# One core, attention and MLP: the same work in another written-out order on every engine

## The chip, the cores and the metric

The kernel runs on one core of a Trainium2 chip. The core has TensorE (PE, matrix products), VectorE (DVE), ScalarE (ACT), GpSimd (POOL) and SyncE (SP). SP computes nothing, it only issues transfers; ACT and POOL can issue transfers too. Each engine works through its own list in order, and a wait for a semaphore at the head of a list holds up all that stands behind it. The metric is the device time of one execution in microseconds.

## The reference

There are two parts. The first is an attention with positive random features, for 8 batches of 8 heads, 576 positions and 64 dimensions:

```
phi(x) = exp(omega x - |x|^2/2 - max) / sqrt(128)      # x = q or k, scaled
kv[m,d] = sum_s phi(k)[s,m] v[s,d];   z[m] = sum_s phi(k)[s,m]
attn[s,d] = phi(q)[s,:] kv[:,d] / (phi(q)[s,:] z + 1e-6)
```

Its output, 4608 tokens of 512 values, goes through an MLP: h = x w_in (512 to 2048), g = h clip(h+3, 0, 6)/6, out = g w_out (2048 to 512). All inputs and the output are float32.

## The kernel before

**Stages.** The program is a list of about 1960 operations, built by `op(...)` calls and numbered in that order. Batches 0 to 7 go through the attention. Of each batch, 512 tokens make one block of the MLP; the 64 left over of every batch are woven into a ninth block (8). TensorE does the attention of one batch while it does the MLP of the block before.

**Names.** An operation's name ends in its batch or block and a number within it. In the attention of batch b and head pair m:

- `k00.b`, `v00.b`, `v10.b`, `ql0.b`, `vl.b` and so on are the loads (line 622). From batch 1 on, k and q are cast to bfloat16 on the way, by loads that POOL issues; v comes as float32 by SP. `castk`, `castq` are the casts of batch 0.
- `T` are TensorE's transposes of k and q in batches 0 and 1 (line 535), `Tev` the copies of their results out of PSUM. From batch 2 on `Tdmak`, `Tdmaq` are transposing transfers on SP's queue (line 748).
- `K`, `Q` are the products with omega in batches 0 to 2 (lines 811, 831). From batch 3 on they come in four bursts `R` a batch, with 64 rows (lines 767, 770). `eK`, `eQ` are the exponentials on ACT, `mx` the maxima on DVE, `cc` their reciprocals.
- `vc`, `vcc`, `vcl` are v and a column of ones scaled by those reciprocals (lines 941 to 949, 857, 860), for the main tokens and the left-over ones. `kv` is the product of phi(k) and v (lines 957, 959), `kvz` its copy, `num`, `rec` and `div` make the quotient (lines 985, 997, 1001).
- `X` turns the quotient on TensorE (line 538) in batches 0 and 1; later `Xdma` (line 1030) and, for the left-over tokens, `Sdma` (line 887) do that on SP's queue.

In the MLP:

- `mm1` is x w_in (line 1054; 1199 for block 0; 1133, in seven products of quarters in place of eight, for blocks 7 and 8), followed by `relu` on ACT and `g` on DVE. In those last blocks `s1`, `s2`, `s3` copy parts of a product within PSUM, `a1`, `a2` add on DVE, and `X1` to `X4` are sums of the inputs.
- `mm2` is g w_out of block 0 (line 1224). From block 1 on it is done in seven products `P1.0` to `P1.6` (the first number is the block, line 1312; 1381 for the last product of block 8). They need sums and differences of g's quarters, `S1` to `S4` (line 1240, nearly all on POOL), and their parts are put together by `p1`, `u2`, `u3`, `C11` to `C22` (ACT or DVE). `out`, `outw`, `outl` are the stores.

w_in comes in pieces `wi0` to `wi3` (line 595), w_out in `wo0` to `wo7` (line 604), through POOL's queue.

**What sets the order.** `ORDER` (line 19) holds one list of operation numbers for each engine, 110 to 550 numbers long. `Prog.schedule` takes the operation at the head of each list, always the one that can begin first by the planner's own clock, and so fixes three things: the program, the PSUM slot (of eight, `Ring`) that an operation gets, and where TensorE's idle fillers (`idle`, line 576, products of ones that nobody reads) stand in the first 21 us. A transfer costs its queue the time `issue` in that clock, and its data share the transfer engines by the weight `packet`. `Prog.emit` then derives the waits from the dependencies. On the chip an engine's list runs in the given order, whatever the clock said. An operation that may run on several engines runs on the one whose list holds its number.

**Gates.** Loads of later batches wait for something that is done by then: those of batch 2 for pieces of w_out (`kb` for wo4, `qb` for wo5, v for wo7), those of batch b from 3 on for products of block b - 2. SP's and POOL's queues hold such a load, and all behind it, until its gate opens.

Of the kernel before, what the change touches and what calls it, by code (L numbers as in the profile page):

```python
# [20 lines left out]
        13, 118, 139, 156, 124, 144, 150, 162, 115, 168, 147, 127, 153, 121, 159, 165, 136, 130, 133, 177, 185, 175,  # L21
        183, 197, 187, 142, 212, 179, 181, 199, 204, 214, 171, 227, 242, 202, 217, 229, 244, 219, 410, 416, 173, 189,
        417, 232, 404, 254, 247, 405, 222, 234, 406, 207, 249, 407, 257, 411, 412, 418, 413, 419, 422, 280, 425, 252,
        237, 260, 428, 300, 431, 434, 437, 440, 286, 284, 282, 443, 318, 306, 303, 288, 446, 449, 309, 312, 452, 298,
        296, 455, 315, 324, 294, 345, 458, 290, 575, 292, 321, 353, 576, 577, 327, 341, 335, 585, 586, 337, 339, 587,
        595, 588, 596, 331, 605, 366, 333, 578, 329, 579, 597, 355, 589, 590, 379, 598, 591, 368, 371, 592, 392, 580,
        581, 343, 606, 599, 381, 358, 607, 384, 600, 582, 394, 397, 601, 374, 608, 361, 609, 602, 387, 400, 610, 611,
        612, 638, 514, 626, 506, 629, 512, 623, 641, 632, 653, 504, 508, 499, 647, 644, 662, 656, 659, 484, 475, 487,
        496, 478, 481, 674, 668, 520, 518, 490, 493, 677, 510, 516, 671, 784, 785, 528, 502, 794, 533, 540, 530, 787,
        545, 542, 800, 564, 552, 788, 717, 554, 795, 569, 566, 557, 797, 798, 697, 801, 803, 804, 710, 807, 808, 811,  # L30
        817, 826, 724, 820, 737, 814, 832, 841, 829, 835, 739, 742, 749, 844, 847, 850, 761, 862, 856, 859, 773, 754,
        865, 778, 766, 751, 972, 988, 775, 973, 763, 982, 975, 976, 983, 885, 985, 986, 989, 898, 991, 992, 1005, 999,
        1014, 1002, 995, 996, 1017, 905, 1008, 1023, 1020, 1029, 925, 1035, 1032, 912, 1038, 1044, 937, 1050, 927,
        1047, 949, 1053, 939, 942, 930, 1160, 1161, 1176, 954, 961, 1170, 966, 951, 963, 1163, 1171, 1086, 1164, 1173,
        1174, 1073, 1177, 1179, 1180, 1093, 1202, 1193, 1190, 1187, 1183, 1184, 1100, 1205, 1196, 1113, 1208, 1217,
        1211, 1118, 1220, 1223, 1125, 1226, 1115, 1137, 1127, 1235, 1130, 1139, 1238, 1232, 1142, 1149, 1241, 1348,
        1349, 1151, 1364, 1154, 1351, 1274, 1352, 1358, 1359, 1281, 1365, 1361, 1362, 1390, 1375, 1378, 1381, 1367,
        1368, 1393, 1371, 1372, 1384, 1405, 1261, 1399, 1414, 1396, 1420, 1411, 1408, 1426, 1301, 1313, 1429, 1303,
        1318, 1306, 1536, 1315, 1423, 1325, 1537, 1288, 1552, 1539, 1540, 1327, 1546, 1330, 1547, 1462, 1337, 1549,
        1342, 1339, 1550, 1553, 1469, 1555, 1556, 1476, 1559, 1560, 1449, 1563, 1569, 1566, 1572, 1581, 1501, 1593,  # L40
        1506, 1503, 1489, 1584, 1525, 1494, 1578, 1491, 1530, 1527, 1513, 1587, 1518, 1596, 1515, 1599, 1602, 1614,
        1608, 1611, 1617, 1631, 1632, 1662, 1675, 1634, 1665, 1691, 1678, 1667, 1635, 1680, 1704, 1670, 1694, 1641,
        1720, 1696, 1683, 1642, 1707, 1699, 1723, 1709, 1733, 1644, 1645, 1725, 1712, 1749, 1736, 1650, 1738, 1728,
        1762, 1752, 1651, 1741, 1754, 1809, 1765, 1647, 1648, 1812, 1767, 1822, 1757, 1654, 1814, 1655, 1770, 1825,
        1817, 1838, 1827, 1778, 1779, 1841, 1851, 1830, 1843, 1867, 1781, 1854, 1782, 1846, 1856, 1880, 1870, 1788,
        1872, 1859, 1883, 1789, 1885, 1909, 1875, 1794, 1896, 1791, 1792, 1888, 1899, 1795, 1912, 1901, 1941, 1914,
        1797, 1798, 1904, 1917, 1801, 1935, 1925, 1926, 1802, 1936, 1928, 1929, 1938, 1939, 1942, 1960, 1957, 1945,
        1946, 1954,
    ],
    "SP": [  # L50
        0, 21, 17, 23, 19, 22, 25, 24, 31, 27, 32, 26, 28, 29, 30, 269, 270, 271, 474, 473, 472, 471, 470, 468, 690,
        469, 402, 614, 584, 694, 696, 594, 693, 695, 692, 604, 536, 548, 560, 572, 691, 573, 881, 878, 810, 883, 879,
        806, 745, 757, 781, 769, 882, 782, 880, 884, 1069, 998, 1072, 1066, 1070, 1071, 994, 1068, 933, 945, 970, 957,
        969, 1067, 1260, 1259, 1257, 1258, 1186, 1133, 1121, 1145, 1157, 1182, 1254, 1158, 1256, 1255, 1374, 1370,
        1447, 1445, 1446, 1448, 1309, 1443, 1333, 1321, 1345, 1444, 1346, 1442, 1509, 1497, 1533, 1521, 1562, 1558,
        1534, 1653, 1657, 1800, 1804, 1953, 1952, 1959, 1962, 1950, 1956,
    ],
    "ACT": [
        18, 20, 117, 119, 157, 145, 151, 163, 132, 169, 148, 129, 154, 193, 166, 196, 160, 178, 211, 184, 137, 176,
        186, 225, 182, 180, 243, 188, 172, 218, 174, 190, 223, 408, 414, 420, 423, 281, 426, 238, 208, 429, 253, 432,  # L60
        301, 435, 438, 441, 283, 285, 444, 261, 319, 307, 304, 447, 310, 450, 313, 289, 299, 352, 297, 325, 346, 316,
        453, 291, 293, 354, 322, 328, 342, 336, 338, 456, 340, 332, 378, 367, 334, 391, 330, 459, 390, 380, 344, 593,
        583, 362, 375, 388, 401, 613, 507, 515, 630, 627, 624, 513, 642, 633, 639, 654, 505, 509, 500, 648, 645, 603,
        663, 657, 660, 476, 497, 482, 479, 485, 675, 488, 494, 519, 669, 491, 523, 511, 672, 517, 503, 529, 539, 678,
        521, 551, 550, 553, 565, 720, 718, 723, 722, 706, 703, 704, 700, 708, 698, 403, 713, 711, 716, 715, 736, 709,
        812, 702, 748, 818, 747, 729, 821, 727, 815, 725, 730, 827, 833, 830, 836, 759, 842, 848, 845, 851, 863, 857,
        774, 860, 866, 974, 977, 897, 894, 891, 896, 892, 888, 886, 899, 890, 903, 921, 901, 1000, 1006, 1003, 923,
        1015, 1018, 906, 936, 904, 1009, 1024, 908, 1021, 911, 1030, 910, 1036, 1033, 913, 574, 915, 1039, 1045, 918,
        938, 1051, 1048, 917, 1054, 959, 960, 962, 1091, 1087, 1092, 1089, 1079, 1084, 1076, 1082, 1074, 1078, 1080,
        1085, 1098, 1099, 1094, 1096, 1194, 1191, 1108, 1203, 1188, 1112, 1111, 1206, 1103, 1197, 1105, 1101, 1209,  # L70
        1212, 1124, 1136, 1218, 1221, 1106, 1224, 1126, 1227, 1138, 1147, 1148, 1239, 1233, 1236, 1242, 1350, 1277,
        1280, 1279, 1275, 1284, 1287, 1282, 1376, 1353, 1379, 1391, 1382, 1286, 1312, 1394, 1385, 1406, 1262, 1270,
        1268, 1266, 1400, 1264, 1415, 1267, 1397, 1297, 1412, 1273, 1409, 1272, 1427, 1324, 1421, 1323, 1430, 1538,
        1424, 1293, 1291, 1289, 1541, 1336, 1294, 1338, 1468, 1465, 1463, 1467, 1474, 1472, 1470, 1159, 1475, 1479,
        1477, 1482, 1481, 1450, 1452, 1458, 1456, 1564, 1455, 1570, 1567, 1454, 1488, 1573, 1502, 1461, 1582, 1460,
        1490, 1585, 1526, 1579, 1514, 1594, 1588, 1597, 1603, 1600, 1609, 1615, 1612, 1618, 1633, 1663, 1664, 1676,
        1677, 1666, 1692, 1679, 1671, 1693, 1636, 1673, 1695, 1684, 1705, 1706, 1686, 1722, 1708, 1700, 1724, 1702,
        1713, 1734, 1735, 1715, 1750, 1737, 1729, 1731, 1753, 1763, 1742, 1764, 1744, 1758, 1810, 1813, 1823, 1760,
        1771, 1824, 1773, 1826, 1818, 1820, 1839, 1831, 1842, 1780, 1852, 1853, 1847, 1833, 1783, 1849, 1860, 1881,
        1882, 1862, 1884, 1876, 1878, 1897, 1889, 1891, 1900, 1913, 1905, 1918, 1907, 1920, 1927, 1930, 1948, 1949,  # L80
        1951,
    ],
    "DVE": [
        16, 12, 11, 15, 14, 5, 138, 4, 9, 140, 10, 125, 7, 158, 146, 116, 191, 152, 164, 6, 122, 128, 149, 155, 194,
        209, 134, 167, 170, 131, 161, 141, 239, 224, 198, 143, 200, 213, 201, 205, 215, 216, 228, 203, 206, 230, 245,
        231, 220, 246, 221, 233, 255, 248, 235, 236, 250, 258, 256, 251, 409, 415, 259, 421, 424, 8, 427, 1623, 430,
# [316 lines left out]
def _emit(nc, es, q, k, v, omega, w_in, w_out, out):  # L403
# [136 lines left out]
    def turned(vx, b, n):  # L540
# [4 lines left out]
       issue=0.4)  # L545
# [67 lines left out]
    def load(b, eng, gates):  # L613
        pb = b % 2
# [3 lines left out]
        def dma(part, dst, src, n, keys, gate, prio, run):  # L618
            cast = b > 0 and part[0] in "kq"
# [4 lines left out]
               name="%s.%d" % (part, b), issue=0.85 if cast else 0.47 if b else 0.52, packet=50.0 if run == 1024 else 18.0)  # L624
# [877 lines left out]
```

The softmax here doesn't subtract the row's maximum and nothing guards it: scores larger than these inputs give would overflow.

## Time and profile before

| quantity | value |
|---|---|
| median of 5 runs | 303.73 us (303.01 to 304.05) |
| profiled execution, its own time | 304.34 us |
| its span, first to last instruction | 302.5 us |
| matmuls on TensorE | 2800, 65 of them fillers |
| granted TensorE clock | 1.00 in every slice |
| VectorE, ScalarE, GpSimd busy | 247.4, 214.3, 237.4 us |
| transposing transfer kT or qT, SP's queue | 1.35 and 1.38 us each, median |
| transposing transfer xT, SP's queue | 1.27 us each, median |
| bytes read and written | 36.73 and 9.44 MB |

In the timelines a row is the start in us, the duration, engine, line, operation, what it writes and reads, the shape and the count; at its end stands the idle time of the engine before it and what released it. SPq and POOLq are the sequencers. Rows of equal operations that follow each other are merged. A matmul's row runs to the end of its result, so that TensorE looks busy between two matmuls whose starts are a little further apart than their columns need.

### The profile page before, as it was taken

The numbers are of one execution on the slowest core, as the hardware profiler recorded it, in microseconds if no ns is written. First come the engines' busy times: TensorE is split into PE (matmuls) and PEld (weight loads), VectorE is DVE, ScalarE is ACT, GpSimd is POOL, SyncE is SP. The second block draws the span as 40 slices with busy tenths as digits, with TensorE's granted clock in tenths as the row PEclk, the third lists the DMA queues.
The fourth block names the chain that finished last, engine by engine and source line by source line (L and its number), as shares of the span: only waits on it lengthen the run. The fifth ranks groups of instructions, "written<-read, shape, count | busy, mean of one in ns | idle before, by whom it ended". The sixth has DMA issues, their size and how long they took to land.

```text
span 302.5 us, 7410 instructions
## 1 busy us (share of the span) xinstructions
PE 296.1 (98%) x2800; PEld 211.0 (70%) x2800; DVE 247.4 (82%) x547; ACT 214.3 (71%) x516; POOL 237.4 (78%) x255
## 2 busy tenths in 40 slices
PE   8999999999999999999999999999999999999995
PEld 5678955545776568655865586657756688888884
DVE  3889897859988794879878967687798999999875
ACT  4898996579949963799479854697686687575400
POOL 2883776069897999799969996998959999999990
PEclk9999999999999999999999999999999999999999
DMA  7999999999994996799949969898932500110034
GB/s 239 286 188 177 265 188 113 194 179 144 221 229 96 137 238 170 154 163 226 177 120 137 161 158 237 114 218 129 134 95 52 168 1 2 69 73 2 0 141 140
DMA packets 90100, 44.89 MB, mean 148 GB/s; under 512 B 57936, under 2 KB 87760, under 8 KB 90064
## 3 DMA queue, kind: packets, MB, share of 16 engines
q1 hardware_dynamic: 62496, 31.04, 45.5%
q0 software_dynamic: 26592, 12.46, 33.7%
q10 hardware_dynamic: 976, 0.92, 0.9%
q8 instruction: 22, 0.36, 0.5%
q14 instruction: 14, 0.11, 0.2%
HBM read 36.73 MB, written 9.44 MB: 153 GB/s over the span
## 4 chain that ended last, share of the span: by engine, by line
PE 90%; ACT 3%; DVE 2%; DMA 2%; POOL 1%; SPq 1%; issue 0%; POOLq 0%
PE p L1312 32%; PE p L1054 28%; PE p L1133 8%; PE p L1224 4%; PE p L985 3%; PE p L1199 3%; PE p L957 3%; PE p L767 2%; DMA q<-in_q_dram 2%; PE p L770 2%; PE p L831 1%; DVE mx L822 1%; PE p L811 1%; ACT kp L818 1%; ACT vc L943 1%; SPq L622 1%
## 5 line engine op out<-in xcount | busy, mean ns | idle before, releaser
L1054 PE MATMUL p<-xT,wi 128*128 128x512 f16 x384 | 89.9, 380 | 0.0
L1062 DVE SCALAR_TENSOR_TENSOR gT<-tsb,p 128x512 f16<-128x512 f16 x96 | 62.2, 676 | 12.8 <-ACT tsb L1060 12.2
L1060 ACT ACTIVATE tsb<-p 128x512 f16<-128x512 f32 x96 | 55.4, 606 | 14.7 <-PE p L1054 8.9
L1054 PEld LDWEIGHTS p<-xT,wi 128*128 128x128 f16 x384 | 35.7, 98 | 38.5 <-issue 1.1
L1312 PE MATMUL p<-wo,gT 128*128 128x256 f16 x368 | 45.3, 273 | 0.0
L1240 POOL TENSOR_TENSOR gT<-gT 128x512 f16<-128x512 f16 x32 | 37.0, 1155 | 3.2 <-DVE gT L1062 0.9
L1312 PEld LDWEIGHTS p<-wo,gT 128*128 128x128 f16 x368 | 34.9, 98 | 6.4 <-issue 1.1
L1240 POOL TENSOR_TENSOR s<-gT 128x512 f16<-128x512 f16 x31 | 36.2, 1168 | 3.9 <-DVE gT L1062 1.7
L1240 POOL TENSOR_TENSOR s<-gT,s 128x512 f16<-128x512 f16 x31 | 35.9, 1156 | 2.6 <-DVE gT L1062 0.3
L1240 POOL TENSOR_TENSOR gT<-gT,s 128x512 f16<-128x512 f16 x30 | 34.7, 1155 | 2.3
L791 DVE TENSOR_REDUCE mx<-kp 128x4 f32<-128x512 bf16 (+1 forms) x50 | 29.7, 622 | 6.5 <-ACT kp L786 6.4
L795 ACT ACTIVATE qpT<-p 128x512 bf16<-128x512 f32 (+1 forms) x50 | 27.5, 571 | 7.7 <-PE p L770 7.1
L622 POOL DMA_DIRECT2D qb<-in_q_dram x28 | 19.6, 716 | 16.4 <-PE p L1054 15.9
L1312 PE MATMUL p<-t,gT 128*128 128x256 f16 x256 | 31.6, 273 | 0.0
L786 ACT ACTIVATE kp<-p 128x512 bf16<-128x512 f32 (+1 forms) x50 | 26.2, 568 | 7.5 <-PE p L770 7.5
L941 POOL TENSOR_TENSOR vc<-v,cc 128x512 bf16<-128x512 f32 x22 | 23.4, 1064 | 10.0 <-DVE mx L822 3.6
L1001 DVE TENSOR_TENSOR xb<-p,rec 128x256 f16<-128x256 f32 (+1 forms) x64 | 28.4, 471 | 0.3
L1312 PEld LDWEIGHTS p<-t,gT 128*128 128x128 f16 x256 | 24.3, 98 | 4.5 <-issue 1.6
L523 ACT COPY p<-p 128x256 f32<-128x256 f32 (+1 forms) x42 | 16.4, 402 | 14.9 <-PE p L1312 8.6
L1181 ACT ACTIVATE tsb<-p 128x512 f16<-128x512 f32 x32 | 18.7, 601 | 8.3 <-PE p L1133 6.2
L1183 DVE SCALAR_TENSOR_TENSOR gT<-tsb,p 128x512 f16<-128x512 f16 x32 | 21.1, 679 | 0.5 <-ACT tsb L1181 0.3
L943 ACT ACTIVATE vc<-v,cc 128x64 bf16<-128x64 f32 x80 | 20.2, 345 | 0.0
(132 smaller groups left out, 586.3 us busy)
## 6 DMA issues: line engine op xcount, KB each, us to landing
v<-in_v_dram SPq DMA_DIRECT2D x14, 512.0 KB, 5.1
out_dram<-osb SPq DMA_DIRECT2D x14, 512.0 KB, 4.0
kb<-in_k_dram POOLq DMA_DIRECT2D x14, 256.0 KB, 4.9
qb<-in_q_dram POOLq DMA_DIRECT2D x14, 256.0 KB, 5.8
wo<-in_moe_w_out_dram POOLq DMA_DIRECT2D x8, 256.0 KB, 9.4
wi<-in_moe_w_in_dram POOLq DMA_DIRECT2D x3, 512.0 KB, 7.4
q<-in_q_dram SPq DMA_DIRECT2D x4, 256.0 KB, 5.6
v<-in_v_dram SPq DMA_DIRECT2D x4, 256.0 KB, 5.5
```

Source lines behind the costliest of these rows:

```text
L786: op("ACT", actt(128 * (d1 - d0)), lambda E, lh=lh, ko=ko, part=part: E.activation(ko, out_of(part, 0, lh)[0].rearrange("p (x m) -> p x m" ...
L791: op("DVE", dvet(128 * (d1 - d0)), lambda E, ko=ko, mo=mo: E.reduce_max(mo, ko, axis=AX.X), p0 + 0.01, reads=[("kp", 0, d, lh) for d in ra ...
L795: op("ACT", actt(128 * (d1 - d0)), lambda E, lh=lh, part=part: E.activation(qd[:, part[0]:part[1], lh, :], out_of(part, 1, lh)[0].rearrang ...
L941: return E.tensor_tensor(vcm[:, :, 0:D], v32[:, m, :, :], cbc, ALU.mult)
L943: ins = E.activation(vcm[:, i, 0:D], v32[:, m, i, :], AF.Copy, scale=cc[pb][:, c0 + i:c0 + i + 1])
L1001: op("DVE", dvet(128 * n), lambda E: E.tensor_tensor(xv(i0, i1), psum()[:, :, :, 0:64], rbc, ALU.mult), t + 0.01, reads=[vn, ("rec", ru)], ...
L1054: ins = E.matmul(ring.t[vh.slot], wi[:, c, 128 * f:128 * f + 128], xv[:, c, :], start=(c == 0), stop=(c == NJ - 1))
L1060: op("ACT", actt(512), lambda E: E.activation(tsb[tu][:], ring.t[vh.slot], AF.Relu, bias=0.5, scale=1.0 / 6.0), t - 0.1, reads=[vh], write ...
L1062: op("DVE", dvet(512), lambda E: E.scalar_tensor_tensor(gT[gu][:, f, :], tsb[tu][:], 1.0, ring.t[vh.slot], ALU.min, ALU.mult), t - 0.1, re ...
L1133: ins = E.matmul(dst, w(c), x[:, c, :], start=start and c == 0, stop=c == 1, skip_group_check=True)
L1240: op(engines, {"POOL": 0.07 + n / 455.0, "DVE": 0.1 + n / 850.0}, lambda E: E.tensor_tensor(dst, x, y, ALU.subtract if minus else ALU.add) ...
L1312: ins = E.matmul(ring.t[v.slot][:, 256 * j:256 * j + 256], a[:, f, 128 * j:128 * j + 128], w[:, f, :], start=(first and f == 0 and j == 0) ...
```

## The change

Five numbers of the planner's clock are replaced: the `issue` times of the loads, of the transposing transfers and of the stores. The five lists of `ORDER` are replaced by others. Every operation but 9 of the fillers is still there, with the same operands. About 70 operations that may run on more than one engine have moved to another one, ACT to POOL, POOL to ACT, DVE to ACT and the reverse among them. The gates and the dependencies stay.

```diff
-               name="%s.%d" % (part, b), issue=0.85 if cast else 0.47 if b else 0.52, packet=50.0 if run == 1024 else 18.0)
+               name="%s.%d" % (part, b), issue=0.85 if cast else 0.62 if b else 0.52, packet=50.0 if run == 1024 else 18.0)
-                       lat=1.0, name="Tdma%s.%d.%d" % (t, b, i), issue=1.2, packet=24.0)
+                       lat=1.0, name="Tdma%s.%d.%d" % (t, b, i), issue=1.5, packet=24.0)
-               name="Sdma.%d" % b, issue=1.2, packet=24.0)
+               name="Sdma.%d" % b, issue=1.35, packet=24.0)
-               group="dxT%d_%d" % (pb, m), inc=16, lat=1.0, name="Xdma" + nm, issue=1.2, packet=24.0)
+               group="dxT%d_%d" % (pb, m), inc=16, lat=1.0, name="Xdma" + nm, issue=1.32, packet=24.0)
-               issue=0.65 if blk == 8 else 0.5, packet=84.0)
+               issue=0.65, packet=84.0)
```

Of the lists, the one of SP as an example. In it 402 is Sdma.1, 690 vl.3, 469 v00.2, and 584, 594, 604, 614 are the stores out.0.0 to out.0.3:

```diff
     "SP": [
-        0, 21, 17, 23, 19, 22, 25, 24, 31, 27, 32, 26, 28, 29, 30, 269, 270, 271, 474, 473, 472, 471, 470, 468, 690,
-        469, 402, 614, 584, 694, 696, 594, 693, 695, 692, 604, 536, 548, 560, 572, 691, 573, 881, 878, 810, 883, 879,
...
+        0, 21, 19, 17, 32, 23, 22, 25, 24, 27, 31, 26, 28, 29, 30, 269, 270, 271, 474, 473, 472, 471, 468, 470, 402,
+        690, 584, 469, 604, 694, 696, 594, 693, 695, 536, 614, 548, 692, 560, 572, 691, 573, 881, 878, 810, 883, 806,
...
```

The places of the other lists that the steps below speak of, by name, before and after:

```
ACT, start      before  castk0.01  Tevk0.01  eK0.4  eK0.0  eK0.2  eK0.6  castq0.0B  eK0.8  eK0.1  castq0.1A  eK0.3  vcl.0  eK0.7 ... vc.0.2
                after   castk0.11  castk0.10  Tevk0.11  eK0.4  eK0.0  eK0.2  eK0.8  eK0.1  castq0.0B  castq0.1A  eK0.3  eK0.5  eK0.6  vcl.0 ... vc.0.2
POOL, 30-48 us  before  wo1 wo0 wo2 wo5 wo3 wo4 wo7  vcl.1  vc.1.0  vcl.1  wo6 ...
                after   wo1 ql1.1 wo0 wo5 wo2  vcl.1  wo3 wo4  vcl.1  wo7  q10.2  vc.1.0  vc.1.1  wo6  vc.1.2 ...
SP, 70-75 us    before  vl.3  v00.2  Sdma.1  out.0.3  out.0.0  Tdmak.3.1 ...
                after   Sdma.1  vl.3  out.0.0  v00.2  out.0.2  Tdmak.3.1 ...
SP, 201-210 us  before  Tdmaq.7.0  Tdmak.7.0  Tdmak.7.1  Tdmaq.7.1 ...
                after   Tdmak.7.0  outw.4.1  vl.7  Tdmaq.7.0  outw.4.0  Tdmak.7.1  Tdmaq.7.1 ...
DVE, end        before  u2.8  S48.3  S48.2  u3.8  C22.8 ...
                after   u2.8  S18.3  S18.2  S48.3  S48.2  u3.8  C11.8  C22.8 ...
```

## The prediction

> **What bounds the kernel now.** I read the page first, then TensorE's own waits, then the places behind them. The first fence is the page (engines, two rows of the 40 slices, the chain that ended last by engine); the second is the list of TensorE's waits; the third TensorE's timeline around 41 us.
>
> ```profile
> PE 296.1 (98%) x2800; PEld 211.0 (70%) x2800; DVE 247.4 (82%) x547; ACT 214.3 (71%) x516; POOL 237.4 (78%) x255
> ...
> PE   8999999999999999999999999999999999999995
> ...
> PEclk9999999999999999999999999999999999999999
> ...
> PE 90%; ACT 3%; DVE 2%; DMA 2%; POOL 1%; SPq 1%; issue 0%; POOLq 0%
> ```
> ```profile
> PE p L957 <- POOL vcl L857: 0.4, 1, 0.4
> ...
> PE p L1312 <- DVE u L1328: 0.4, 1, 0.4
> ```
> ```profile
> 40.05 0.59 PE L1224 MATMUL p<-wo,gT 128*128 128x512 f16 x2
> ...
> 41.54 0.42 PE L957 MATMUL p<-vc,kp 128*128 128x65 bf16 x8 [0.45 <-POOL vcl L857]
> ```
>
> TensorE is full from the second slice to the last, its clock is at its most, and the chain is 90% TensorE. So a new order can win only (a) before about 20 us, where line 576 still puts 65 fillers into holes, (b) at TensorE's few waits, (c) in the last 3 us. "Busy" hides short waits, so I took the steps between matmul starts. After 20 us they exceed the streaming time by more than 60 ns at about 45 places, 5.4 us in all. 41 are the changes into and out of the 64-row bursts (lines 767, 770), about 97 ns each in any order. The remaining five come to 1.5 us: 0.61 before kv.1.0 (41.54), 0.52 before P1.3 (87.56), 0.21 before kv.6.2 (205.53), 0.11 and 0.09. That is the whole gain that the middle can give; a loss has no such bound, since many producers end just in time (below).
>
> **Part by part.** *The changed constants* (0.47 to 0.62, 1.2 to 1.5, 1.35 and 1.32, 0.5 to 0.65) only steer the planner's own clock. What they set on the chip is which PSUM slot an operation gets, where fillers stand (56 for 65), and what is waited for. Fillers stand in holes; each is 0.11 us if one is late. Cost 0.
>
> *Start.* The new order gives casts and transposed copies of batch 0 to other engines. This is ScalarE's timeline:
>
> ```profile
> 10.89 0.59 ACT L818 ACTIVATE kp<-p 128x512 bf16<-128x512 f32 x1
> 12.39 1.05 ACT L860 ACTIVATE vcl<-vl,cc 64x65 bf16<-64x65 f32 x4 [0.91 <-DVE cc L935]
> ...
> 17.15 2.04 ACT L943 ACTIVATE vc<-v,cc 128x64 bf16<-128x64 f32 x8
> ```
>
> The eight copies at 17.15 (vc.0.2) release kv.0.2 at 19.25, from where TensorE is full. In the new order ScalarE does castk0.10 first, which waits for a load that lands at about 6.45, so its exponentials begin at about 7.45 instead of 6.42: 1.0 late. But two of them (eK0.5, eK0.6; a further one costs 0.48) stand ahead of vcl.0 and fill the 0.91 hole, Tevq0.1B (0.48) has gone to VectorE, and 0.5 of single waits for loads goes. Counted operation by operation with these durations, vc.0.2 begins at about 16.2, 0.95 earlier, and kv.0.2, the first turns of x and mm1 follow by about 1.0. VectorE, which gains three copies, ends div.0.3B at about 22.6 (24.5 now), so it doesn't take this back.
>
> TensorE can't keep it all. The first mm2 (line 1224, 40.05 now) needs the w_out piece that lands at 39.4, and weights and k, q, v of batch 1 queue behind each other from 10 to 47 us, so this landing hardly moves with the start. The new order has the same load second, behind 64 KB more. Kept: 40.05 - 39.4 = 0.65. If the load follows the start, up to 1.0; if it comes 0.65 later, nothing.
>
> *41.54.* kv.1.0 waits for the second vcl.1 on GpSimd, which stands behind vc.1.0, and that behind the load v10.1 (lands 39.2). The new order puts both vcl.1 ahead of vc.1.0 and kv.1.0 some 4 us of TensorE work later: the 0.61 goes. What is put there: the cast load q10.2 now stands ahead of vc.1.0 in GpSimd's queue, gated by wo5, third of the w_out pieces (the third lands at 40.6 now). GpSimd then issues q10.2 (0.73), does vc.1.0 (1.05) and is ready at 42.5; kv.1.0 wants it at about 44.0. Behind it are vc.1.1, wo6 and vc.1.2, with 1 us of margin each, and vc.1.3 with about 0.5. Cost 0; each 1 us more of landing beyond 42.1 would cost up to 1.
>
> *SP's queue at 71 us.* SP's queue, GpSimd's and TensorE's:
>
> ```profile
> 71.33 0.51 SPq L622 DMA_DIRECT2D v<-in_v_dram  x1
> 71.88 1.18 SPq L887 DMA_TRANSPOSE xs<-xb  x1
> 73.10 1.05 SPq L1234 DMA_DIRECT2D out_dram<-osb  x2
> ```
> ```profile
> 77.13 0.23 POOL L949 TENSOR_TENSOR vc<-ones,cc 128x8 bf16<-128x8 f32 x1
> 78.30 2.23 POOL L941 TENSOR_TENSOR vc<-v,cc 128x512 bf16<-128x512 f32 x2 [0.94 <-POOL vc L949]
> ```
> ```profile
> 79.41 0.43 PE L957 MATMUL p<-vc,kp 128*128 128x65 bf16 x8
> ```
>
> The load at 71.33 (v00.2) takes 6.9 us and lands at 78.2; GpSimd has stood idle for 0.94 and starts vc.2.0 at once, which ends at 79.35, and kv.2.0 starts at 79.41. Slack 0.06, and S21.3 behind it on GpSimd (85.66) meets P1.2 (85.73) as closely. The new order puts the store out.0.0 (256 KB) ahead of v00.2. Such a store's data take 0.77 in this queue (80.51 - 79.74, the landings of two that follow each other). kv.2.0 is also asked for 0.1 later, and the small load kl.3, which runs against v00.2, starts 1.2 earlier. So kv.2.0 stalls 0.5: none if the data of the two pass each other, 0.9 if nothing helps. [...] The row has every landing of this queue here in order of issue, so I take 0.5.
>
> *Rest of the SP queue.* In blocks 2 to 7 loads, transposes (1.2 to 1.5 us each) and stores swap places, but transposes keep their gates. I moved each by what passes it: the four xT transposes land 1.8 to 3.6 us ahead of mm1, qT and kT 1.9 to 12 ahead of their burst, moved by at most 1.6. Tdmaq.7.0 goes behind Tdmak.7.0, a store and a load (2.6 later), yet kl.7, its gate, is issued earlier: about 1 us is left. Cost 0.
>
> *Middle.* Swaps among 1900 operations and some 70 moved evacuations, additions and v scalings (ACT to POOL, POOL to ACT, DVE to ACT) change arrivals by up to 0.5 us. Where I followed them (114 to 124, 134 to 153, 194 to 224 us) slacks stayed between 0 and 0.5. kv.2.2, kv.2.3, kv.6.2 and kv.5.0 have 0.06 to 0.27 now. Bounds: -0.3 (the small waits go) and +1.5 (three new ones like that at 41.54); taken +0.2.
>
> *End.* S18.2 and S18.3 go from GpSimd to VectorE, C11.8 as well. GpSimd's and VectorE's timelines:
>
> ```profile
> 287.46 1.16 POOL L1240 TENSOR_TENSOR s<-gT 128x512 f16<-128x512 f16 x1
> ...
> 288.24 0.66 DVE L1240 TENSOR_TENSOR s<-gT 128x512 f16<-128x512 f16 x1
> 288.70 1.21 POOL L1240 TENSOR_TENSOR s<-gT,s 128x512 f16<-128x512 f16 x1
> 288.93 1.26 DVE L1240 TENSOR_TENSOR s<-gT,s 128x512 f16<-128x512 f16 x1
> ...
> 293.22 2.08 DVE L1240 TENSOR_TENSOR gT<-gT,s 128x512 f16<-128x512 f16 x2 [1.06 <-PE p L1312]
> ```
>
> GpSimd is unbroken from 229 to 295 and now runs 2 us ahead there: no gain, TensorE doesn't wait. VectorE gets two sums. By the short row 0.66 each, 1.3, against a hole of 1.06: +0.1 at most after C11.8 (0.6, against a hole of 0.55 ahead of 298.48). [...] Taken +0.1, bounds 0 and +0.7. The three last stores move from SP to ACT: 0.57 and 0.58 to issue, the same.
>
> Sum: -0.65 - 0.61 + 0.5 + 0.2 + 0.1 = -0.46. The profiled execution took 304.34 (span 302.5 and 1.8 around it), 0.2% over the median of 303.73; the difference goes onto the median: 303.3.
>
> **Rivals.** *Full gain*: w_out follows the start and v00.2 passes the store: -1.0 - 0.61 + 0.1 = 302.2. For it: v00.2 has 0.5 us of helpers. Against it: the DMA row stands at 9 through these slices.
>
> *Slower by the v load*: its landing doesn't move with TensorE's lead, because the DMA queues are full, and stays at 78.2 + 0.8 = 79.0. vc.2.0 then ends at 80.2, and TensorE, 1.26 ahead, wants it at 79.41 + 0.1 - 1.26 = 78.3: a stall of 1.9 instead of 0.5. -1.26 + 1.9 + 0.3 = +0.94, 304.7. It decides from a landing of 78.1 on; up to there something of the lead is left. For it: the 6.9 us of the load; against it: the queue was empty when SP issued it.
>
> *It does nothing*: lead and stalls cancel, 303.7.
>
> **How the numbers follow.** Changes of under 0.2% (0.6 us) can't be told from none here. Sum as worked 0.40, half of it beyond 303.1; full gain 0.18; slower 0.32 (304.3 to 305.4, also for a new wait elsewhere); nothing 0.10. Faster 0.20 + 0.18 + 0.02 = 0.40, same 0.20 + 0.05 = 0.25, slower 0.32 + 0.03 = 0.35. The likeliest alone spans 302.6 to 303.9; the range, 301.9 to 305.2.
>
> **What would show it.** Right: vc.0.2 at about 16.2; no wait ahead of kv.1.0; the first mm2 waiting for w_out at 39.4; an idle stretch of about 0.5 at kv.2.0; a full TensorE from 229 on. Wrong: fillers or line 1199 no earlier than now; GpSimd waiting for wo5 beyond 42; TensorE waits of 0.3 and more in blocks 2 to 6; a gap ahead of P8.62.

## The result

The changed kernel takes 304.93 us (median of 44 executions, 303.66 to 307.12), the kernel before 303.9 (79 executions). The ratio is 1.0037, with an interval of 1.0027 to 1.0048. So the change costs about 1.1 us, where a gain of 0.5 was forecast.

The profiled execution took 306.56 us (span 304.6). That is 1.6 over the median, so part of what its trace shows is the loss of this one execution.

First the page of the changed kernel: engines, the slices of TensorE and its clock, the chain that ended last.

```profile
PE 297.4 (98%) x2791; PEld 212.3 (70%) x2791; DVE 245.3 (81%) x542; ACT 219.1 (72%) x532; POOL 231.6 (76%) x251
...
PE   7999999999999999999999999999999999999994
...
PEclk9999999999999999999999999999999999999999
...
PE 91%; DMA 4%; DVE 2%; POOL 1%; SPq 1%; ACT 0%; issue 0%
```

TensorE bounds the kernel as before. Two things differ: the first slice is down from 8 to 7 (a run below with the start of before, `b_tail`, has 7 too), and the chain now has 4% DMA in place of 2%, 3% of it the load of w_in (its row of the chain by line is "DMA wi<-in_moe_w_in_dram 3%"). Next TensorE's waits in the changed kernel:

```profile
...
PE p L1054 <- ACT qpT L795: 0.5, 1, 0.5
PE p L1312 <- DVE u L1328: 0.3, 1, 0.3
...
```

The 0.4 us for `vcl` (the wait at kv.1.0) is no longer listed; one of 0.5 us for an exponential on ScalarE is new. The steps between matmul starts give four new or changed waits beyond the streaming time: 0.30 before mm1.0A.12 (28.91, for the load wi3), none before kv.1.0, 0.41 before R5.1 (149.66; 0.10 there in before) and 0.62 before mm1.5.8 (187.22). Followed at equal work, TensorE is behind the first trace of before by 0.73 us at 25 us, 1.03 at 29 to 39, 0.42 at 45, 0.39 at 96 to 120, 0.71 at 151, 1.44 at 190 and 1.28 at its last matmul.

The rest of the loss comes after TensorE has finished. These are the timelines of VectorE and of the queues at the end, first of the kernel before, then of the changed one:

```profile
297.44 0.49 DVE L1389 TENSOR_TENSOR osb<-p,u 128x128 f32<-128x128 f32 x2
297.76 1.21 SPq L1392 DMA_DIRECT2D out_dram<-osb  x2
...
299.20 0.54 SPq L1408 DMA_DIRECT2D out_dram<-osb  x1
299.35 0.42 DVE L1389 TENSOR_TENSOR osb<-p,u 128x256 f32<-128x256 f32 x1 [0.18 <-PE p L1381]
299.81 0.58 SPq L1392 DMA_DIRECT2D out_dram<-osb  x1
```
```profile
299.29 0.49 DVE L1389 TENSOR_TENSOR osb<-p,u 128x128 f32<-128x128 f32 x2
299.61 1.46 ACTq L1392 DMA_DIRECT2D out_dram<-osb  x2
...
300.64 0.42 DVE L1389 TENSOR_TENSOR osb<-p,u 128x256 f32<-128x256 f32 x1 [0.18 <-PE p L1381]
301.11 0.85 ACTq L1408 DMA_DIRECT2D out_dram<-osb  x1
302.00 0.61 ACTq L1392 DMA_DIRECT2D out_dram<-osb  x1
```

In both, VectorE takes up the last addition (C12.80) 0.03 to 0.04 us after TensorE's last matmul ends. Before, its data are ready at 299.77 and the store is issued at 299.81. Now they are ready at 301.06 and the store is issued at 302.00: ACT's queue is still working through the three stores ahead of it. From the end of TensorE's last matmul to the end of the span, 3.21 us have become 4.03. I call this stretch "the end" below.

### The profile page after: what moved, and what is told of

It is laid out like the page before. It is cut to its first block, busy times and chain, and to the rows that moved or that the text cites. A ratio compares the mean times of both kernels' runs of the same rounds, so it can differ in the third digit from the quotient of the medians.

```text
span 304.6 us, 7385 instructions
## 1 busy us (share of the span) xinstructions
PE 297.4 (98%) x2791; PEld 212.3 (70%) x2791; DVE 245.3 (81%) x542; ACT 219.1 (72%) x532; POOL 231.6 (76%) x251
## 4 chain that ended last, share of the span: by engine, by line
PE 91%; DMA 4%; DVE 2%; POOL 1%; SPq 1%; ACT 0%; issue 0%
PE p L1312 30%; PE p L1054 27%; PE p L1133 8%; PE p L1224 5%; PE p L1199 3%; PE p L985 3%; PE p L957 3%; DMA wi<-in_moe_w_in_dram 3%; PE p L576 2%; PE p L811 2%; PE p L767 2%; PE p L831 2%; PE p L770 1%; PE p L535 1%; DMA xs<-xb 1%; SPq L1030 1%
## 5 line engine op out<-in xcount | busy, mean ns | idle before, releaser
L1060 ACT ACTIVATE tsb<-p 128x512 f16<-128x512 f32 x96 | 54.7, 605 | 10.5 <-PE p L1054 9.3
L1240 POOL TENSOR_TENSOR gT<-gT 128x512 f16<-128x512 f16 x30 | 34.6, 1154 | 2.4 <-DVE gT L1062 0.2
L941 POOL TENSOR_TENSOR vc<-v,cc 128x512 bf16<-128x512 f32 x21 | 22.0, 1047 | 14.4 <-DVE cc L935 7.4
L523 ACT COPY p<-p 128x256 f32<-128x256 f32 (+1 forms) x49 | 18.6, 398 | 13.8 <-PE p L1312 7.4
L1312 PEld LDWEIGHTS p<-t,gT 128*128 128x128 f16 x256 | 24.2, 98 | 4.1 <-issue 0.8
L943 ACT ACTIVATE vc<-v,cc 128x64 bf16<-128x64 f32 x88 | 22.3, 350 | 1.1 <-DVE cc L935 1.1
L1181 ACT ACTIVATE tsb<-p 128x512 f16<-128x512 f32 x32 | 18.1, 599 | 6.2 <-PE p L1133 4.0
```

The lines of the kernel that those rows point to most:

```text
L941: return E.tensor_tensor(vcm[:, :, 0:D], v32[:, m, :, :], cbc, ALU.mult)
L943: ins = E.activation(vcm[:, i, 0:D], v32[:, m, i, :], AF.Copy, scale=cc[pb][:, c0 + i:c0 + i + 1])
L1060: op("ACT", actt(512), lambda E: E.activation(tsb[tu][:], ring.t[vh.slot], AF.Relu, bias=0.5, scale=1.0 / 6.0), t - 0.1, reads=[vh], write ...
L1240: op(engines, {"POOL": 0.07 + n / 455.0, "DVE": 0.1 + n / 850.0}, lambda E: E.tensor_tensor(dst, x, y, ALU.subtract if minus else ALU.add) ...
L1312: ins = E.matmul(ring.t[v.slot][:, 256 * j:256 * j + 256], a[:, f, 128 * j:128 * j + 128], w[:, f, :], start=(first and f == 0 and j == 0) ...
```

## The experiments

Twelve executions of a kernel (ten of `b_c118`) give its ratio to about 0.15 to 0.35%, so a part of half a microsecond is read from the trace, and the ratios only say whether the parts add up. Each ratio is against the kernel before on the same chip.

**The three places, undone one at a time in the changed kernel.** First, `a_stores`: the nine last stores go back to the queues that they had before.

```diff
 SP:  ..., outw.8.0, outw.8.0,
-     outw.8.1, outw.8.1
+     outl1, outl2, outw.8.1, outl0
 ACT:
-     outw.8.1, outl2, outl1, outw.8.1, outl0
+     outw.8.1, outw.8.1, outw.8.1
```

> The changed kernel with the nine last stores on the queues of before (outl0 to outl2 and one outw.8.1 from ACT back to SP). Theory: four stores behind each other on ACT cost 0.6 to 0.85 us of issue each, so the last is issued 0.94 us after its data; back on SP it is issued at once, the time from TensorE's last matmul to the end falls from 4.3 to 3.5 us and the median to 304.1. Rival: VectorE's later sums set the end and the queues are alike; under 0.2 us.

(What was run is the diff: one outw.8.1 goes back from SP to ACT, and the 4.3 of this text is 4.03 by the measure used here.)

Measured: ratio 1.0043 (1.0019 to 1.0067), median 305.25. The end is 3.71 us. So 0.32 of the 0.82 are the stores' queue; the median can't resolve that. Another 0.5 is left, since VectorE is late with C12.81 and C12.82: they begin 1.31 us before TensorE's last matmul ends, 1.88 in the trace of before. The stores of these two, and the two behind them on the same queue, follow. The timeline of `a_stores` shows it: four stores on SP almost without a gap, the last still 0.6 us after its data.

```profile
298.75 1.20 SPq L1392 DMA_DIRECT2D out_dram<-osb  x2
...
299.99 0.60 SPq L1408 DMA_DIRECT2D out_dram<-osb  x1
300.63 0.61 SPq L1392 DMA_DIRECT2D out_dram<-osb  x1
```

There are four stores behind each other in the changed kernel too, so the 0.32 isn't their number. They take longer to issue on ACT: 1.46, 0.85 and 0.61 us in the rows above against 1.20, 0.60 and 0.61 in `a_stores`, 0.5 in all; 0.2 of it is lost again, as the first of the four comes 0.2 later in `a_stores`, counted from the end of TensorE's last matmul. The seven traces with the changed end all have 0.87 to 0.88 and 0.84 to 0.86 for ACT's second and third of these stores; the ten with them on SP have at most 0.64. Why they are longer there isn't shown. It isn't ACT by itself: where ACT's queue is empty at that point, a store like the third takes it 0.55 to 0.57, and with the changed end one of SP's stores takes 0.83 to 0.85 as well.

Second, `a_tail`: the whole end as before.

```diff
 (a_stores, and)
-DVE:  u2.8, S18.3, S18.2, ..., u3.8, C11.8, C22.8
+DVE:  u2.8, ..., u3.8, C22.8
-ACT:  p1.8, outw.8.1
+ACT:  p1.8, C11.8, outw.8.1
-POOL: S28.2, S48.0
+POOL: S28.2, S18.2, S18.3, S48.0
```

> The changed kernel with the whole end of before: the nine last stores on its queues, C11.8 on ScalarE, S18.2 and S18.3 on GpSimd. Theory: VectorE's added work (C11.8 0.67 us, two sums) makes C12.81 and C12.82 0.57 us later against TensorE's last matmul, so their stores and the two behind them; undone together with the stores, the time from TensorE's last matmul to the end of the span is 3.2 us as in before (4.03 in the changed kernel, 3.71 with the stores alone). Median 304.1. Rival: the stores alone were the cause and the rest of the difference is the landing of the last store; it stays at 3.7 and the median at 304.6.

Measured: ratio 1.0005 (0.9978 to 1.0032), median 304.47 beside 304.49 for before on that chip. The end is 3.20 us. Its timeline, to be laid beside those of before and of `a_stores`:

```profile
297.78 1.20 SPq L1392 DMA_DIRECT2D out_dram<-osb  x2
299.17 0.54 SPq L1408 DMA_DIRECT2D out_dram<-osb  x1
299.78 0.58 SPq L1392 DMA_DIRECT2D out_dram<-osb  x1
```

Third, `a_mid`: two moves in the middle undone. They are what the traces name behind the waits at 149.66 and 187.22. On GpSimd's and SP's queues of the changed kernel:

```profile
131.31 0.81 POOL L622 DMA_DIRECT2D kb<-in_k_dram  x1
```
```profile
132.58 1.09 SPq L1408 DMA_DIRECT2D out_dram<-osb  x2
141.75 1.36 SPq L748 DMA_TRANSPOSE kT<-kb  x1
143.22 2.82 SPq L748 DMA_TRANSPOSE qT<-qb  x2
```

The load at 131.31 is k00.5. It was the first of its batch on GpSimd (125.75) and is now behind the scaling vc.4.1; its data come at 141.73 in place of 130.27. SP's Tdmak.5.0 waits for it, so SP's queue stands from 133.7 to 141.75, and Tdmaq.5.0 behind it lands at 149.57, which is what R5.1 waits for. The other move is Swv.5, ScalarE's copy of a leftover transpose. Here are ScalarE and TensorE of the changed kernel:

```profile
185.97 0.77 ACT L523 COPY xS<-xs 128x256 f16<-128x256 f16 x1 [2.16 <-DMA xs<-xb]
186.49 0.68 ACT L795 ACTIVATE qpT<-p 128x512 bf16<-128x512 f32 x1
```
```profile
187.22 2.12 PE L1054 MATMUL p<-xT,wi 128*128 128x512 f16 x9 [0.46 <-ACT qpT L795]
```

Swv.5 was done at 218 before. Now it keeps ScalarE standing for 2.16 us and holds eQ6.10.0 behind it, for which mm1.5.8 waits.

```diff
-POOL: kl.5, k10.5, q00.5, q10.5, vc.4.1, k00.5
+POOL: k00.5, kl.5, k10.5, q00.5, q10.5, vc.4.1
-ACT:  eK6.10.0, Swv.5, eQ6.10.0, ..., relu.5.0
+ACT:  eK6.10.0, eQ6.10.0, ..., relu.5.0, Swv.5
```

> The changed kernel with two moves undone: the load k00.5 first of its batch in GpSimd's queue again, and Swv.5 behind relu.5.0 on ScalarE in place of ahead of eQ6.10.0. Theory: k00.5 (issued 131.3 in place of 125.8, landing 141.7 in place of 130.3) holds SP's queue until 141.7 and so Tdmaq.5.0 until 149.57; Swv.5 holds ScalarE for Sdma.5 until 185.95. With both back R5.1 (0.41) and mm1.5.8 (0.62) don't wait, TensorE ends 1.0 us earlier and the median is 303.9. Rival: the next producers are as late; a wait of like size appears behind each place and the median stays above 304.5.

Measured: ratio 1.0026 (1.0008 to 1.0044), median 304.89. Both waits are gone and nothing takes their place; the end keeps its 4.03. But the other runs that still have both moves limit what they are worth: `a_fill`, `a_start`, `a_tail`, `a_wi3` and `a_fill2` show neither wait, `a_stores` one of 0.39 near 188 us, put down to another copy on ScalarE that waits for a store. Over the seven traces with both moves in place that is 0.41 + 0.62 + 0.39 = 1.42, or 0.2 us a trace. The changed kernel's profiled execution happened to show both at once. The times, too, point to a price that some executions pay: with both moves in place (the changed kernel and six runs here) 24 of 116 executions took over 306.5 us, with both moved back (`a_mid`, and `a_best` and `a_tail_mid` below) none of 36.

**The end in the kernel before.** `b_tail` is the reverse of `a_tail`: the order of before with the changed end.

```diff
 (the three lists of a_tail and the stores of the changed kernel,
  in the order of before)
```

> The kernel before with the end of the changed one: the nine last stores on its queues, C11.8, S18.2 and S18.3 on VectorE. Theory: the end costs 0.8 us by itself: from TensorE's last matmul to the end 4.0 us in place of 3.2, and the median 0.8 us up. Rival: in the company of before's other orders VectorE has room and the end grows by less than 0.3.

Measured: ratio 1.0031 (1.0015 to 1.0047), median 304.93 beside 303.78. The end is 4.05 us, as expected. Its additions on VectorE and its stores on ACT:

```profile
297.36 1.46 ACTq L1392 DMA_DIRECT2D out_dram<-osb  x2
...
298.39 0.43 DVE L1389 TENSOR_TENSOR osb<-p,u 128x256 f32<-128x256 f32 x1 [0.18 <-PE p L1381]
298.86 0.86 ACTq L1408 DMA_DIRECT2D out_dram<-osb  x1
299.76 0.61 ACTq L1392 DMA_DIRECT2D out_dram<-osb  x1
```

The last data are ready at 298.82 and their store waits 0.94 us, the same number as in the changed kernel. The end alone, put into before, costs nearly all that the change costs.

`b_c118` asks which of the moves to VectorE counts.

```diff
-ACT:  p1.8, C11.8, outw.8.1
+ACT:  p1.8, outw.8.1
-DVE:  u3.8, C22.8
+DVE:  u3.8, C11.8, C22.8
```

> The kernel before with one move: C11.8 from ScalarE to VectorE, behind u3.8, as in the changed kernel. The forecast's step: 0.6 us against a hole of 0.55 ahead of C21.8, so +0.1 at most. Theory: C12.81 and C12.82 stand ahead of that hole; they and their two stores come 0.6 us later, the two stores behind them on SP with them, and from TensorE's last matmul to the end it is 3.7 us in place of 3.2. Rival: VectorE's sums S18.2 and S18.3 were what made it late; it stays at 3.2 to 3.3.

Measured: ratio 0.9999 (0.9979 to 1.002), the end 3.42 us: 0.2, between the two expectations. So, if the parts add up, the 0.82 are about 0.2 for C11.8, 0.3 for the two sums (what is left of the 0.5; no run moves them alone) and 0.3 for the stores' queue. C12.81 begins 1.48 us ahead of the end of TensorE's last matmul in place of 1.88, so it is 0.4 later; SP's queue, which stood idle for 0.3 us between its last stores before, takes up part of that.

**The start.** `a_start` puts everything that began before 24 us back into the order of before, 65 fillers included.

```diff
-ORDER, every engine: the changed list
+ORDER, every engine: what began before 24 us as in before, then the changed list
```

> The changed kernel with the order of before for every operation that began before 24 us in the trace of before (all engines; 65 fillers then). If the start's order (with or without the clock) costs what the traces show, 1.0 us of lead at 29 to 39 us, the median falls by 0.6 to 1.0 us, to 303.9 to 304.3, and the spread is that of before. Rival: the loads that arrive at 39 to 41 us take it back, and the median stays at 304.9.

Measured: ratio 1.0054 (1.0019 to 1.0089), median 305.11; the end is 4.03. By this, and by `a_tail`, which has the changed start and is level with before, the changed start isn't the loss. The trace of `a_start` has TensorE's last matmul begin at 298.28, 0.76 ahead of the first trace of before, but that trace turns out to be no good zero (below).

`a_wi3` issues the load wi3 ahead of two of the loads of k.

```diff
-POOL: vc.0.3, kl.1, k00.1, wi3, k10.1
+POOL: vc.0.3, wi3, kl.1, k00.1, k10.1
```

> The changed kernel with the load wi3 issued on GpSimd ahead of kl.1 and k00.1 in place of behind them (1.5 us of issue earlier). Theory: wi3 (landing 28.3 to 28.9 us, 27.8 in before) is what takes the start's gain back: the wait ahead of mm1.0A.12 (0.3 to 0.9 us) goes, and TensorE is 0.3 to 0.9 us further at 30 us. Rival: the landing is set by the full queues and hardly moves, or k of batch 1 is late for its casts in its place; no gain at 45 us.

Measured: ratio 1.0042 (1.0022 to 1.0062). This is the rival's case. wi3 now lands at 25.02 and isn't waited for, but k00.1 lands at 27.10 in place of 24.2 to 25.8 in the other traces with this start, and a transpose of batch 1 waits for it: 1.15 us beyond the streaming time at 25.78. The waits of TensorE in `a_wi3`, then in `a_tail`, which has the changed start as it is, and `a_tail`'s timeline:

```profile
PE p L535 <- DMA kb<-in_k_dram: 1.0, 1, 1.0
```
```profile
PE p L1199 <- DMA wi<-in_moe_w_in_dram: 1.5, 1, 1.5
```
```profile
28.54 1.70 PE L1199 MATMUL p<-xT,wi 128*128 128x256 f16 x14 [1.45 <-DMA wi<-in_moe_w_in_dram]
```

In `a_tail` TensorE is 1.0 us ahead of before at 25 us, as the forecast said of the new start. It then waits 1.62 us for wi3 and is 0.66 behind. Five of the other traces with this start wait for wi3 as well, 0.30 to 0.92 us. The lead itself isn't in every trace: without the runs that add fillers it is 0.97, 0.98 and 0.84 in `a_tail`, `a_tail_mid` and `a_wi3`, 0.37 in `a_stores`, 0.04 in `a_mid`, and TensorE is 0.73 behind in the changed kernel's own trace. The nine traces with the start of before lie between 0.28 behind and 0.42 ahead. With one load moved ahead the next one is late: from 20 to 29 us the DMA row of `a_tail` stands at 9 in nearly every slice, so I read this as a limit of the transfers together and not of one place in the queue.

**Half speed.** In the changed kernel's profile TensorE runs at half its rate until 10.2 us, though the table by stretches (`--windows`) gives its granted clock as 1.00 there. Its rows, then those of before:

```profile
7.54 1.06 PE L811 MATMUL p<-om,kT 128*128 128x256 bf16 x4
...
10.30 0.38 PE L811 MATMUL p<-om,kT 128*128 128x256 bf16 x2
```
```profile
5.99 0.39 PE L811 MATMUL p<-om,kT 128*128 128x256 bf16 x2 [0.20 <-ACT kT L523]
6.22 0.39 PE L535 MATMUL p<-ident,kb 128*128 128x128 bf16 x4
6.44 0.60 PE L811 MATMUL p<-om,kT 128*128 128x256 bf16 x4
```

Four matmuls of 256 columns take 1.06 us in the first and 0.60 in the second (steps of 214 and 109 ns). TensorE's first matmul is at 1.19 us in these traces. Its first step at full speed comes 3.0 to 6.2 us later in 16 of the 17 and 9.1 us later in this one. That the waits of 0.36, 0.31 and 0.50 us between 5.0 and 6.7 us hold it back, and the 8.3 us of the next text, were guesses of mine, which no trace shows. `a_fill` put fillers into these waits.

```diff
-PE: Tk0.01, (omega), Tk0.l, Tk0.11, K0.4
+PE: Tk0.01, (omega), idle, Tk0.l, idle, Tk0.11, idle, idle, K0.4
```

> The changed kernel with four more fillers in TensorE's queue: one ahead of Tk0.l, one ahead of Tk0.11, two ahead of K0.4 (its waits of 0.36, 0.31 and 0.50 us at 5.42, 5.87 and 6.72). Theory clock: those waits keep TensorE at half speed (steps of 214 ns for 256 columns) until 10.2 us. Filled, full speed comes by 8.3 us at the latest, vc.0.2 begins about 0.7 us earlier (17.1), the upper group of times (305.5 to 307.1) goes, and the median falls by 0.4 to 0.7 us, to about 304.4. Rival order: the start is late because its casts and copies stand in a worse order, and half speed only fills waits; vc.0.2 stays at 17.8 and the median at 304.9.

Measured: ratio 1.0066 (1.0034 to 1.0098). The run tells nothing: these fillers were of the second group, which waits for a load of k (k00.0, landing 7.09), so they made one gap of 2.1 us in place of filling three. `a_fill2` has fillers without that gate.

```diff
 (a_fill, and)
-            idle_work(IDLE[1], 0.11, [("k32", 0, 0)])
+            idle_work(IDLE[1], 0.11, [])
```

> The first filler run again, with fillers that wait for no load: one ahead of Tk0.l and Tk0.11 each, two ahead of K0.4. If the waits between 5.0 and 6.7 us are what can hold TensorE at half speed, full speed comes by 7 us, and no run of the group above 306.5 is left (the changed kernel has 5 of 44 there); the median falls by 0.2 to 0.4 us, to 1.003 or less. If that one half-speed start was no matter of the waits, ratio 1.0037 as it was.

Measured: ratio 1.0049 (1.0019 to 1.0078), and 4 of 12 executions above 306.5. The first step at full speed comes at 6.9 us, but traces of this start whose waits are not filled have it as early (5.9 us in `a_stores` and `a_tail`, 7.4 in `a_mid`). Only the one execution had it at 10.3. No run shows the half-speed start to be a part of the 0.37%; what sets its length is left open.

**The terms of the forecast, one move each in before.** `b_again` is before, unchanged.

> The kernel before, unchanged, as a measure of what twelve executions can tell and as a second trace of it. Both theories expect a ratio of 1.000 within 0.002. If the first trace of before (304.34 us) was a slow one, the span is 301.9 to 302.2 here; if it was typical, 302.5.

Measured: ratio 1.0013 (0.9996 to 1.003), profiled execution 304.29 us. The span is 302.5 again, yet not by the same waits. This trace has no wait at kv.1.0 and one of 0.88 beyond the streaming time for wi3. Its timeline of TensorE:

```profile
27.38 0.38 PE L811 MATMUL p<-om,kT 128*128 128x256 bf16 x2
28.48 1.69 PE L1199 MATMUL p<-xT,wi 128*128 128x256 f16 x14 [0.72 <-DMA wi<-in_moe_w_in_dram]
...
41.29 0.38 PE L811 MATMUL p<-om,kT 128*128 128x256 bf16 x2
41.51 0.42 PE L957 MATMUL p<-vc,kp 128*128 128x65 bf16 x8
```

The kernels that have before's order there give the spread of two landings (in `b_vcl`, the next run, the wait is for vc.1.0 alone):

| trace | wi3 lands | wait | v10.1 lands | wait at kv.1.0 |
|---|---|---|---|---|
| before | 27.76 | none | 39.19 | 0.61 |
| `b_again` | 28.34 | 0.88 | 38.85 | none |
| `b_v00` | 27.54 | none | 37.82 | none |
| `b_tail` | 26.68 | none | 37.54 | none |
| `b_c118` | 28.50 | 1.17 | 38.32 | none |
| `b_vcl` | 27.84 | none | 40.21 | 0.95 |

The two waits stand in for each other: in `b_again` and `b_c118` the wait for wi3 had put TensorE 0.6 and 0.8 us behind by 39 us, so that kv.1.0 was asked for later.

`b_vcl` makes the move that the forecast took for the cure of kv.1.0.

```diff
-POOL: vcl.1, vc.1.0, vcl.1, wo6
+POOL: vcl.1, vcl.1, vc.1.0, wo6
```

> The kernel before with one move: GpSimd's second vcl.1 ahead of vc.1.0 in place of behind it. Theory: the wait ahead of kv.1.0 (0.61 us at 41.54) was vcl.1's place alone; it goes, nothing takes it back, TensorE ends 0.5 to 0.6 us earlier, median lower by 0.5 us. Rival: vc.1.0 or a w_out piece is late next at the same place; TensorE gains under 0.2 us.

Measured: ratio 1.0005 (0.9992 to 1.0019), median 303.93. In its profiled execution v10.1 landed at 40.21, and kv.1.0 waited 0.95 us for vc.1.0 itself. So the rival holds: with this landing there is a wait without vcl.1, whose place only adds to it.

`b_kv1` takes the changed order for what began between 27 and 50 us.

```diff
-ORDER, every engine: the list of before
+ORDER, every engine: what began from 27 to 50 us in the changed order, the rest as in before
```

> The kernel before with the changed order only for what began between 27 and 50 us (both vcl.1 ahead of vc.1.0, kv.1.0 later, the w_out loads in their new order). Theory: the wait of 0.61 us at kv.1.0 goes and nothing takes it back; TensorE is 0.6 us ahead from 45 us to the end, median 303.3. Rival: a landing or a producer behind it takes it back; the lead is gone by 100 us and the median is 303.9.

Measured: ratio 1.0032 (1.0005 to 1.006). The border at 50 us spoilt it: it left a vc.1 product behind three loads on GpSimd, and a kv product waits 0.74 us for it at 52.21. The wait at kv.1.0 was gone, the 0.7 was new, and the sum says nothing of the full change, which has no such wait.

`b_v00` puts the store ahead of the load v00.2.

```diff
-SP: vl.3, v00.2, Sdma.1, out.0.3, out.0.0
+SP: vl.3, out.0.0, v00.2, Sdma.1, out.0.3
```

> The kernel before with one move: the store out.0.0 ahead of the load v00.2 in SP's queue. The forecast's step: v00.2 lands 0.8 us later (79.0), GpSimd's vc.2.0 is late by it and TensorE stalls 0.5 us (0 to 0.9) at kv.2.0, and is 0.5 us later to the end. Rival: data of a store and of a load pass each other, the landing moves by less than 0.2 and TensorE doesn't stall.

Measured: ratio 1.0009 (0.9992 to 1.0025), median 303.99. In the trace a wait is there. v00.2 lands at 78.44 and kv.2.0 waits; TensorE's timeline:

```profile
77.74 1.47 PE L1312 MATMUL p<-wo,gT 128*128 128x256 f16 x12
79.66 0.43 PE L957 MATMUL p<-vc,kp 128*128 128x65 bf16 x8 [0.44 <-POOL vc L941]
```

It is 0.61 beyond the streaming time, and TensorE's place against the first trace of before goes from 0.34 ahead to 0.26 behind and stays there. That the store's data hold the load up isn't shown. v00.2 takes 6.91 us from issue to landing here; in the six traces without the store ahead of it (before, `b_again`, `b_vcl`, `b_c118`, `b_kv1`, `b_tail`) it takes 5.89 to 7.04, and in the ten with the changed order there 5.56 to 6.69. What the store does cost is 0.5 us of issue: v00.2 is issued 0.95 us after vl.3 in place of 0.41.

**What the places add up to.** `a_best` takes before's start and end and the two moves of `a_mid`; the order from 24 to 285 us is the changed one.

```diff
 (a_start, a_tail and a_mid together)
```

> The changed kernel with the start of before (until 24 us), k00.5 and Swv.5 moved back, and the end of before; what is left of the change is its order from 24 to 285 us. Theory of four places (start and wi3 0.5, k00.5 and Swv.5 0.4 to 1.0 when they bite, end 0.8, and 0.6 gained at kv.1.0): TensorE ends 0.8 us earlier than in before (298.5), the tail is 3.2, the median 303.2 to 303.4, below before. Rival: the many swaps in the middle cost by themselves in most executions; median 304.0 or more.

Measured: ratio 1.0012 (0.9993 to 1.0032), median 304.24, end 3.21. It is no faster than before. `a_tail_mid` leaves the changed start in.

```diff
 (a_tail and a_mid together)
```

> The changed kernel with the end of before and with k00.5 and Swv.5 moved back; its own start and the rest of its order stay. If the end and those two places are the whole loss, the ratio to before is 1.000 within 0.002 and the end is 3.2 us; if the start or the rest gains what the forecast said (0.65 and 0.61), the ratio is 0.996; if they lose, above 1.002.

Measured: ratio 0.9997 (0.9975 to 1.002), median 304.30 beside 304.13. With the end and the two places taken back the whole rest of the new order, start and some 1900 operations, is worth nothing measurable either way, to within about 0.7 us. No version here is shown to beat before.

The end in all traces is the firmest reading, since it hardly moves from one to the next:

| kernels | end, us |
|---|---|
| before, `b_again`, `b_vcl`, `b_v00`, `b_kv1`, `a_tail`, `a_best`, `a_tail_mid` | 3.20 to 3.22 |
| `b_c118` | 3.42 |
| `a_stores` | 3.71 |
| changed, `a_fill`, `a_fill2`, `a_start`, `a_mid`, `a_wi3`, `b_tail` | 4.03 to 4.05 |

## Why the prediction was wrong, by its steps

The step that failed first is *End*: "taken +0.1, bounds 0 and +0.7", and in it "the three last stores move from SP to ACT: 0.57 and 0.58 to issue, the same". It measured 0.82, above its bound. The issue wasn't the same: the last four stores took 1.46, 0.85 and 0.61 us on ACT and 1.21, 0.54 and 0.58 on SP. I counted the work moved to VectorE against the hole ahead of C21.8, where TensorE is waited for. C12.81 and C12.82 stand ahead of that hole and have stores of their own. And I took the last store as hidden while nothing lies behind it: it is issued 0.94 us after its data in place of 0.04, and 0.82 of these 0.90 came out in the end. Nor does the short row of 0.66 give the price of a sum of VectorE. In the two profiles eight of its ten sums after 288 us (line 1240) start while one of GpSimd's is running; each of them ends 0.28 us after GpSimd's and takes 0.52 to 1.41 us, while the other two take 0.41 and 0.42. The bound of +0.7 was an estimate; no run moves the two sums alone.

The step *Start* (-0.65) was wrong about the load, and right about TensorE in some traces only. Its sign, vc.0.2 at about 16.2, came in `a_tail`, `a_wi3` and `a_tail_mid` (16.1 to 16.2, with a lead of 0.8 to 1.0 us at 25 us); in the changed kernel's own trace vc.0.2 began at 17.77. I held the lead against the w_out piece at 39.4, for which no trace waits, but the next load that TensorE asks for is wi3, 11 us earlier; it takes the lead back, in `a_tail` more than all of it. I had asked what stands ahead in each engine's list and not, of every load in the stretch, when it lands against when it would be wanted.

The step *41.54* (-0.61) took one execution for the rule: of the five traces with GpSimd's order of before there, one has the wait. The changed kernel's trace had none, as forecast, and still nothing was gained in the median.

The step *SP's queue at 71 us* (+0.5) came out in size in `b_v00` (0.61), but not by its mechanism: 0.5 us of issue went ahead of the load, and that the 0.77 of the store's data did isn't shown. So the runs don't decide between the 0 and the 0.5 that I weighed there. In the changed kernel the term was absent, since TensorE was 0.4 us behind and v00.2 landed at 78.61. Of the other traces with this part of the change, only `a_fill2` waits there by 0.1 us or more (0.29, at 78.77); `b_kv1` waits 0.19 without it.

*Rest of the SP queue*, "Cost 0", and *Middle*, "+0.2": I moved each transpose by what passes it in SP's queue, but the delay came from GpSimd, whose load k00.5 gates it, and from one copy on ScalarE that waits for SP. The bounds (-0.3 to +1.5) held the 1.03 of the profiled execution. The average of 0.2 over seven traces is what was taken, by luck: none of the places named for it is where the loss came.

*The changed constants and fillers*, "Cost 0": no run measures them alone; `a_tail_mid` holds them all and comes out at 0.9997.

Summed again: start 0, kv.1.0 0, v00.2 0, middle +0.2, end +0.8, together +1.0 where 1.1 is measured. So of the 1.5 us between forecast and result the end is 0.7, the start and kv.1.0 are 0.65 and 0.61 that were never gained, and the 0.5 of v00.2 that didn't come goes the other way. The rival "slower by the v load" had the right side and nearly the right time, 304.7, by the wrong mechanism, which is luck.

## What to carry to other kernels

The end of this kernel hid no store (0.82 us of the 0.90 above came out), so count the stores on each queue from the last data backwards, issue by issue (0.54 to 0.88 us each here), and let the last one find its queue empty. Take a wait for a transfer in one trace as a draw, not as a price: look at a second trace of the same kernel before counting it as a gain. And when TensorE is made earlier, list every load of that stretch with its landing; the first one that lands late is where the gain ends.

## What was not expected of the hardware

The same load in the same order landed at very different times from one execution to another: v10.1 at 37.54 to 40.21 in the six of the table. For k00.5 the seven traces with both moves fall into two groups. Issued at 129.5 to 129.7 us, it landed at 135.3 to 136.1 in four; issued at 130.8 to 131.3, it landed at 139.9 to 141.7 in three. In these three the two stores behind it on SP's queue were issued 1.25 to 1.35 us after it, in the other four 1.77 to 2.25. About 1 us of later issue went with 4 to 6 us of later landing, so this spread isn't pure chance. That the stores are the reason isn't shown.

The long executions go with the two moves of the middle (24 of 116 and 0 of 36, above). They are not their only source: `b_kv1`, which has before's order at both places, has 3 of 12 over 306.5 us, and before reaches 306.62.

TensorE's half-speed start had ended by 7.4 us in all traces but one, and at 10.3 us in that one, with the granted clock shown as 1.00 in that one too. It was seen in the steps between matmuls (214 ns for 256 columns against 109).
